# Pooled attention and a channel mix on one core: another way to take the row maximum from head 14 on, and six pieces of work on other engines

## The chip, the cores and the metric

The kernel runs on one core of a Trainium2 chip. The metric is the device time of one execution in microseconds; for the kernel before there are three runs. The profile is of one more execution, taken by the hardware profiler. TensorE does the matrix products (PE, and PEld for its weight loads), VectorE is DVE, ScalarE is ACT, GpSimd is POOL, and SyncE (SP) issues all transfers.

## The reference

Inputs: q, k, v of 8 batches x 8 heads x 1152 rows x 64, and the weights of a channel mix (512 x 1024, 1024 x 512, 512 x 512).

```
q_pool = q.reshape(B, H, S // 2, 2, D).mean(axis=3)          # 576 rows
scores = scale * q_pool @ k.T                                # 576 x 1152
attn = exp(scores - max(scores)); attn /= sum(attn) + 1e-9
x = (attn @ v), heads side by side                           # 8 x 576 x 512
xk = mu_k * x + (1 - mu_k) * x_prev ; xr likewise with mu_r
out = sigmoid(xr @ w_r) * ((relu(xk @ w_k) ** 2) @ w_v)
```

The result is wanted at float32 accuracy, so most operands are kept as two 16-bit parts, a high and a low one.

## The kernel before, in words

64 heads are taken one after the other; each is cut into 6 blocks of 96 pooled queries, 384 blocks in all. `prep` loads k and v of a head, splits k into a high and a low part (`kn`, L521 and L524), turns them by a DMA transpose into `ks1`, and copies the high part into the lower half of `ks2`. It also makes the parts of v (`vt`) and a scaled copy (`vb`, L552 on ScalarE for the first 8 heads, L555 on GpSimd after that).

A block (`block`, L562) has one of three PSUM buffers `s` of 1024 columns: 128 scratch columns and 9 x 96 scores, keys on the partitions, queries on the columns. Its steps:

1. 9 products with `ks1` (L583).
2. VectorE takes the maximum over the 9 key chunks, per partition and query (L590), to `mx`.
3. TensorE transposes `mx` by a product of 128 columns into the scratch (L593); VectorE takes the maximum over 128 keys (L595), to `mb`.
4. TensorE brings the 96 maxima back onto one row by a product with a diagonal (L602, 96 columns); ScalarE writes that row, pushed a little so that it bounds from above, into row 0 of the low part of q (L605).
5. 9 products with `ks2`, whose row 0 holds a constant and so subtracts the maximum (L599).
6. ScalarE's exponential, to `pf` (L611); GpSimd makes the low plane `pl` (L619).

`window` and `halves` multiply the planes with v (L640, L669, L671, L676) and divide by the row sums to `xb`. Two heads together are turned so that features lie on the partitions: for pairs 4 to 30 (`crossed`) GpSimd splits `xb` into 16-bit planes `xp` (L719), a DMA transposes them to `xd`, and ScalarE (first 64 tokens) and GpSimd (the rest) join them to `xt` (L730).

When a batch of 8 heads is done its channel mix follows (`ff`), in 18 tiles of 256 tokens over the whole run: `mix` makes the mixed tokens `xm` (L884), a high part on ScalarE (L889) and a low part on VectorE (L892), then come the products (L913; 256 columns against w_k, 512 against w_r and w_v), three for each pair of operands. The weights are decoded into two parts in the first 8 heads or so (`weights`, L772 to L802).

No loop sets the order of work. Every operation is entered into a list with an engine, a duration, what it reads and writes, and a key (`Issue.add`); a planner plays the list with these durations, sorts by the resulting start times, shifts some priorities at random by the seeds in `MOVES`, and issues every engine's work in that fixed order. So each engine runs its own queue in order, and the second half's products fill TensorE's time between blocks.

Of the kernel before, what the change touches and what calls it, by code (L numbers as in the profile page):

```python
# [11 lines left out]
F32 = mybir.dt.float32  # L12
# [25 lines left out]
EPS = 2.0 ** -10  # L38
ROW = "Prelu"
CROSS = range(4, 31)  # L40
SPLIT_ENG = "POOL"
JOIN_ENG = "POOL"
HALF_ENG = 'ACT'
CROSS_LOAD, CROSS_MORE = 2.1, 0.5


# [9 lines left out]

LATE, SLACK = 0.04, 0.05
KN_POOL = 0
XL_POOL = 0
DEC_K, DEC_RV = "V", "V"  # L60
ALT = 0
PL_ENG, PL_N = (), 0
VB_ACT = 8
HALF = 1.02
PE_T = 2
N_KN = 3
WR_AT = 5
WV_AT = 6
DEC_V = "Y"
# [14 lines left out]
WDEP = [("ks1", 1), ("ks2", 0), ("vr", 1)]  # L84
AHEAD2 = 0
MOVES, BASE, REACH = (
    19, 49, 186, 236, 290, 409, 442, 580, 720, 1033, 1106, 1276, 1618, 2283, 5078, 5201, 6339, 9039, 9106,
    9116, 10203, 12147, 12598, 14335, 15483, 18964, 19207, 19294, 19356, 20563, 27506, 27677, 27810,
), 2000000, 1150.0
SEED, SPREAD = 37, 1.0  # L90


class Issue:
# [1 line left out]
    LAT = {("PE", "DMA"): 0.2, ("PE", "PE"): 0.0,  # L95
           ("PE", "ACT"): 0.26, ("PE", "DVE"): 0.23, ("DVE", "PE"): 0.17, ("ACT", "PE"): 0.17,
           ("ACT", "POOL"): 0.18, ("DVE", "POOL"): 0.155, ("POOL", "PE"): 0.11, ("ACT", "DVE"): 0.142,
           ("DVE", "ACT"): 0.128, ("DVE", "DVE"): 0.12, ("ACT", "ACT"): 0.13, ("POOL", "POOL"): 0.13}
    ISSUED, LANDED, AHEAD = 1.2, 0.45, 8.0

    def __init__(self):
# [216 lines left out]
def kernel(  # L318
# [78 lines left out]
    xm = bufs("xm", 3, [P, T], F32)  # L397
# [32 lines left out]
    def later():  # L430
        for x, t_ in enumerate(ks2):
# [127 lines left out]

    BK = [(0, 4), (4, NC)]  # L560

    def block(n, j, i, t):  # L562
# [10 lines left out]
        mxz, mbz, y = mx[i % 2], mb[z], i % 2  # L573
# [12 lines left out]
        for c0, c1 in BK:  # L586
            op("PE", (c1 - c0) * 0.0430, lambda c0=c0, c1=c1: scores(c0, c1),
               r=[("ks1", hp), ("ks1", hp, 5)] + kh, w=[("s", z)], key=t)

        op("DVE", 0.975, lambda: nc.vector.tensor_reduce(mxz[:, P - QN:P], grid(0, NC).rearrange("p c q -> p q c"),  # L590
                                                         axis=AX.X, op=ALU.max),
           r=[("s", z)], w=[("mx", y)], key=t)
        op("PE", 0.059, lambda: nc.tensor.matmul(s[:, 0:P], mxz, identb, start=False, stop=False, skip_group_check=True),  # L593
           r=[("mx", y)], w=[("s", z)], key=t + O_MAX)
        op("DVE", 0.199, lambda: nc.vector.tensor_reduce(mbz, s[:, 0:P], axis=AX.X, op=ALU.max),  # L595
           r=[("s", z)], w=[("mb", z)], key=t + O_MAX)
# [5 lines left out]
        op("PE", 0.047, lambda: nc.tensor.matmul(s[:, 0:QN], mbz.broadcast_to([P, P]), negi[:, P - QN:P],  # L602
                                                 start=False, stop=False, skip_group_check=True),
           r=[("mb", z)], w=[("s", z)], key=t + O_MAX)
        op("ACT", 0.153, lambda: nc.scalar.activation(qlo[0:1], s[0:1, 0:QN], getattr(AF, ROW),  # L605
                                                      scale=1.0 - EPS, alpha=(1.0 + EPS) / (1.0 - EPS)),
           r=[("s", z)] + kl, w=qm, key=t + O_MAX)
        for c0, c1 in BK:
            op("PE", (c1 - c0) * 0.0430, lambda c0=c0, c1=c1: scores2(c0, c1),
               r=[("ks2", hp)] + kl + qm, w=[("s", z)], key=t + O_EXP)  # L610
        op("ACT", NC * QN / 1200 + 0.06, lambda: nc.scalar.activation(  # L611
            pf[:, :, rows], grid(0, NC), AF.Exp, bias=SHIFT, scale=0.125 / (2.0 * SQ)), r=[("s", z)], w=[("pf", x) for x in us] + [("gate", i)], key=t + O_EXP)
        pe = PL_ENG[i % len(PL_ENG)] if i < PL_N else "POOL"
        if pe == "ACT":
            op(pe, NC * QN / 1200 + 0.09, lambda: nc.scalar.activation(
                pl[:, :, rows], half(pf, U16, 0)[:, :, rows], AF.Copy, scale=LO), r=[("pf", x) for x in us], w=[("pl", x) for x in us], key=t + O_REST)
        else:
            en, d = (nc.gpsimd, NC * QN / 1000 + 0.12) if pe == "POOL" else (nc.vector, NC * QN / 1920 + 0.07)
            op(pe, d, lambda: en.tensor_scalar(  # L619
                pl[:, :, rows], half(pf, U16, 0)[:, :, rows], LO, 1.0, op0=ALU.mult, op1=ALU.mult),  # L620
               r=[("pf", x) for x in us], w=[("pl", x) for x in us], key=t + O_REST, port=True)
# [246 lines left out]
    def mix(w, t0, t1, key, dk, y):  # L868

        m, o = mu[w]  # L870
        n = t1 - t0
        for c in range(NG):
            t, zx = t0, turn("xm", 3)
            x_m, kx = xm[zx], [("xm", zx, False), ("xm", zx, True)]
            while t < t1:
                b = t // TQ
                e = min(t1, (b + 1) * TQ)
                x, s0, ln, o0 = xt[b % 3], t - b * TQ, e - t, t - t0
                z = turn("tmp")
# [113 lines left out]
    for n in range(B * H):  # L993
# [70 lines left out]
```

## Time and profile before

| | us |
|---|---|
| median of 3 runs | 1112.23 |
| lowest, highest | 1108.02, 1112.65 |
| profiled execution, its own time | 1112.57 |
| profiled execution, span from first to last instruction | 1110.4 |

The span is what the views of the profile divide; the 2.2 us beside it lie before the first and after the last instruction. An instruction's duration in a view is its own, from start to end. Neighbours on one engine can overlap, matmuls above all, whose ends are modelled, so a sum of durations can exceed an engine's busy time.

### The profile page before, as it was taken

To read this page: it belongs to the slowest core of one execution; us is meant where nothing else is said; L and a number is where in the kernel's file an instruction comes from. 1 tells how busy PE (TensorE), PEld (TensorE's weight loads), DVE (VectorE), ACT (ScalarE), POOL (GpSimd) and SP (SyncE) were. 2 spreads that over 40 slices of the span, in tenths; PEclk is the share of its full clock that TensorE was granted. 3 is DMA by queue.
4 is the path that set the end of the run, shared out by engine and by line. 5 is a ranking of instruction groups with operands and counts; after the bars stand their busy time and mean duration, and the time that the engine had idled before them with its cause. 6 is when DMAs were issued, how large, how long until landed. Compare 5 with 4: busy or idle time off the path is not lost.

```text
span 1110.4 us, 44176 instructions
## 1 busy us (share of the span) xinstructions
PE 1070.5 (96%) x18821; PEld 877.6 (79%) x18821; DVE 905.3 (82%) x1632; ACT 836.8 (75%) x1767; POOL 615.9 (55%) x632
## 2 busy tenths in 40 slices
PE   6778899999999999999999999999999999999998
PEld 5777788978798787988797978888797978787565
DVE  7998879988888988899988889897878888874530
ACT  7999987877877777777777777777777777766643
POOL 4656775764566563655565555655565656653111
PEclk9999999999999999999999999999999999999999
DMA  9997837464766655566576566756465554410000
GB/s 228 244 222 191 203 89 144 94 130 98 176 131 127 141 116 137 110 141 125 131 140 139 107 126 116 131 119 134 112 125 102 133 101 78 88 40 11 20 24 25
DMA packets 254165, 134.52 MB, mean 121 GB/s; under 512 B 189456, under 2 KB 226320, under 8 KB 253968
## 3 DMA queue, kind: packets, MB, share of 16 engines
q1 hardware_dynamic: 253968, 131.71, 55.6%
q8 instruction: 147, 2.41, 0.9%
q14 instruction: 50, 0.41, 0.1%
HBM read 67.11 MB, written 9.44 MB: 69 GB/s over the span
## 4 chain that ended last, share of the span: by engine, by line
PE 62%; DMA 2%; DVE 1%; ACT 1%; issue 1%; POOL 0%; SPq 0%; ACTq 0%; DVEq 0%
PE f L913 25%; PE s L583 8%; PE s L599 8%; PE s L913 4%; PE a L676 4%; PE a L671 4%; PE a L669 4%; PE a L913 2%; PE a L640 2%; PE s L593 1%; DMA ks<-kn 1%; DMA qT<-qn 1%; PE s L602 1%; ACT pf L611 1%; DVE mx L590 0%
## 5 line engine op out<-in xcount | busy, mean ns | idle before, releaser
L619 POOL TENSOR_SCALAR pl<-pf 128x864 f16<-128x864 uint16 x384 | 383.3, 998 | 320.8 <-ACT pf L611 264.6
L590 DVE TENSOR_REDUCE mx<-s 128x96 f16<-128x864 f32 x384 | 400.2, 1052 | 79.8 <-PE s L583 36.5
L611 ACT ACTIVATE pf<-s 128x864 int32<-128x864 f32 x384 | 335.4, 882 | 84.3 <-PE s L599 62.5
L583 PE MATMUL s<-qT,ks 128*128 128x96 f16 x3456 | 217.4, 207 | 15.1 <-ACT pf L611 14.0
L599 PE MATMUL s<-qT,ks 128*128 128x96 f16 x3456 | 212.5, 206 | 3.8 <-ACT qT L605 3.0
L583 PEld LDWEIGHTS <-ks 128*128 128x128 f16 x3456 | 182.2, 98 | 41.6 <-issue 19.2
L599 PEld LDWEIGHTS <-ks 128*128 128x128 f16 x3456 | 177.0, 98 | 23.7 <-issue 5.8
L671 PE MATMUL a<-vt,pf 128*128 128x64 f16 x2304 | 192.5, 194 | 0.0
L669 PE MATMUL a<-vt,pf 128*128 128x65 f16 x2304 | 192.0, 193 | 0.0
L669 PEld LDWEIGHTS <-pf 128*128 128x128 f16 x2304 | 161.9, 99 | 4.5
L671 PEld LDWEIGHTS <-pf 128*128 128x128 f16 x2304 | 155.1, 97 | 6.5
L605 ACT ACTIVATE qT<-s 1x96 f16<-1x96 f32 x384 | 88.1, 232 | 89.9 <-PE s L602 82.8
L913 PE MATMUL f<-xhk,wk_hi 128*128 128x256 f16 x496 | 135.2, 273 | 1.0 <-ACT r L940 0.5
L913 PE MATMUL f<-xhk,wk_lo 128*128 128x256 f16 x496 | 135.2, 273 | 0.0
L913 PE MATMUL f<-xlk,wk_hi 128*128 128x256 f16 x496 | 135.2, 273 | 0.0
L595 DVE TENSOR_REDUCE mb<-s 128x1 f16<-128x128 f32 x384 | 108.4, 285 | 31.0 <-PE s L593 27.2
L944 POOL TENSOR_TENSOR gl<-g 128x512 f16<-128x512 f32 x72 | 77.9, 1082 | 84.6 <-ACT g L942 70.1
L676 PE MATMUL a<-vb,pl 128*128 128x65 f16 x2304 | 124.3, 193 | 0.0
L913 PEld LDWEIGHTS <-wk_hi 128*128 128x128 f16 x1152 | 105.5, 98 | 11.4 <-issue 1.2
L676 PEld LDWEIGHTS <-pl 128*128 128x128 f16 x2304 | 98.7, 98 | 5.4
L913 PE MATMUL f<-wv_hi,g 128*128 128x512 f16 x240 | 91.0, 379 | 0.0
L913 PE MATMUL f<-wv_hi,gl 128*128 128x512 f16 x240 | 90.9, 379 | 0.0
(119 smaller groups left out, 2028.8 us busy)
## 6 DMA issues: line engine op xcount, KB each, us to landing
kr<-in_k_dram SPq DMA_DIRECT2D x64, 288.0 KB
vr<-in_v_dram SPq DMA_DIRECT2D x64, 288.0 KB
qr<-in_q_dram SPq DMA_DIRECT2D x63, 256.0 KB
ks<-ks SPq DMA_DIRECT2D x64, 144.0 KB
out_dram<-em SPq DMA_DIRECT2D x36, 256.0 KB
xt<-in_moe_w_k_dram SPq DMA_DIRECT2D x8, 512.0 KB
xt<-in_moe_w_v_dram SPq DMA_DIRECT2D x8, 512.0 KB
qr<-in_q_dram SPq DMA_DIRECT2D x32, 64.0 KB
```

What stands on the lines that cost most here:

```text
L583: nc.tensor.matmul(cols(c, c + 1), ks1[hp][:, c, :], qhi, start=(c == c0), stop=False, skip_group_check=True)
L590: op("DVE", 0.975, lambda: nc.vector.tensor_reduce(mxz[:, P - QN:P], grid(0, NC).rearrange("p c q -> p q c"), axis=AX.X, op=ALU.max), r=[( ...
L595: op("DVE", 0.199, lambda: nc.vector.tensor_reduce(mbz, s[:, 0:P], axis=AX.X, op=ALU.max), r=[("s", z)], w=[("mb", z)], key=t + O_MAX)
L599: nc.tensor.matmul(cols(c, c + 1), ks2[hp][:, c, :], qlo, start=False, stop=True, skip_group_check=True)
L605: op("ACT", 0.153, lambda: nc.scalar.activation(qlo[0:1], s[0:1, 0:QN], getattr(AF, ROW), scale=1.0 - EPS, alpha=(1.0 + EPS) / (1.0 - EPS) ...
L611: op("ACT", NC * QN / 1200 + 0.06, lambda: nc.scalar.activation(pf[:, :, rows], grid(0, NC), AF.Exp, bias=SHIFT, scale=0.125 / (2.0 * SQ)) ...
L619: op(pe, d, lambda: en.tensor_scalar(pl[:, :, rows], half(pf, U16, 0)[:, :, rows], LO, 1.0, op0=ALU.mult, op1=ALU.mult), r=[("pf", x) for ...
L669: nc.tensor.matmul(bank[:, a0:a0 + VN], half(pf, F16, 1)[:, c, rows], vt[jv][:, c, D:D + VN], start=(w == 1 and c == 0 and hh == 0), stop= ...
L671: nc.tensor.matmul(bank[:, a0:a0 + D], half(pf, F16, 1)[:, c, rows], vt[jv][:, c, 0:D], start=False, stop=False, skip_group_check=True)
L676: nc.tensor.matmul(bank[:, a0:a0 + VN], pl[:, c, rows], vb[jv][:, c, 0:VN], start=False, stop=(c == NC - 1), skip_group_check=True)
L913: nc.tensor.matmul(ps, terms[i][0], terms[i][1], start=(first and i == 0), stop=(i == last), skip_group_check=True)
L944: op("POOL", 2 * n * 0.00203 + 0.08, lambda f2=f2: nc.gpsimd.tensor_tensor(gl[:, f2, 0:n], g32[:, f2, 0:n], gh[:, f2, 0:n], op=ALU.subtrac ...
```

## The change

From head 14 on (`N_ROW = 14`) steps 2 to 4 of a block are replaced. VectorE takes the maximum with 32 x 32 transposition over each group of 32 queries in one instruction (`top`), which leaves for each group of 32 partitions the maximum over its 32 keys. `join` then does the rest: a maximum over the key chunks (9 numbers to 3), a product with a mask that spreads the four partition groups over 6 columns, one TensorE product of 18 columns with the constant `gather`, which brings the four groups onto 32 partitions, a maximum over two windows of 5 columns (the maximum and its positive part), and VectorE's 32 x 32 transposition straight into rows 0 to 31 of the low part of q. `ks2` now has a constant in rows 0 and 1; ScalarE's step is gone in these blocks. Heads 0 to 13 keep the old steps with the new constants.

Besides: the split and the joins of `crossed` are on ScalarE (`SPLIT_ENG`, `JOIN_ENG`); the scaled v of all heads is on ScalarE (`VB_ACT`); the low parts of the mixed tokens are on GpSimd (`XL_POOL`); `kn` has two buffers (`N_KN`); the fills of `ks2` are done by VectorE at the start and no longer by GpSimd under a key; the planner gets a few other durations, another seed and other moves. `PAIR = 99` means that the joining of two blocks at once is not used.

```diff
-SPLIT_ENG = "POOL"
-JOIN_ENG = "POOL"
+N_ROW = 14
+PAIR = 99
+SPLIT_ENG = 'ACT'
+JOIN_ENG = 'ACT'
...
-XL_POOL = 0
+XL_POOL = 9999
-VB_ACT = 8
-HALF = 1.02
+VB_ACT = 99
+HALF = 0.92
+XM_D = 0.126
-N_KN = 3
+N_KN = 2
...
-SEED, SPREAD = 37, 1.0
+SEED, SPREAD = 7, 1.0
...
+    mask = const.tile([P, 6], F32, name="mask")
+    gather = const.tile([P, P // U, U], F16, name="gather")
+    nc.vector.memset(mask, 0.0)
+    for a in range(P // U):
+        part = slice(a * U, (a + 1) * U)
+        nc.vector.memset(mask[part, a + 1:a + 2], 1.0 / SM)
+        nc.gpsimd.tensor_copy(gather[part], ident[part, part].unsqueeze(1).broadcast_to([U, P // U, U]))
+    nc.vector.memset(mask[0:U, 0:1], 1.0 / SM)
...
-            op("POOL", 0.6, lambda t_=t_: nc.gpsimd.memset(t_[0:D], 0.0), w=[("ks2z", x)], key=60.0)
-            op("POOL", 0.9, lambda t_=t_: nc.gpsimd.memset(t_[0:1], SM), w=[("ks2z", x), ("ks2", x)], key=60.0)
+    for t_ in md:
+        nc.gpsimd.memset(t_, 0.0)
+    for t_ in ks2:
+        nc.vector.memset(t_[0:D], 0.0)
+        nc.vector.memset(t_[0:2], -SM * 2.0 * EPS)
+        nc.vector.memset(t_[0:1], -SM * (1.0 - EPS))
...
+        def top(y, a):
+            op("DVE", 0.972, lambda: nc.vector.tensor_reduce(
+                my[y][:, a], cols(0, NC).rearrange("p (x q) -> p x q", q=U), axis=AX.X, op=ALU.max, apply_transpose=True),
+               r=[("s", z)], w=[("my", y)], key=t)
+
+        def join(y, m):
...
+            op("DVE", 0.062 + 0.028 * m, lambda: nc.vector.tensor_reduce(
+                mr.rearrange("p (a j) -> p a j", j=3), my[y][:, 0:m].rearrange("p a (c j) -> p a j c", j=3), axis=AX.X, op=ALU.max),
+               r=[("my", y)], w=[("s", z)], key=t + O_MAX)
+            op("DVE", 0.061 + 0.019 * m, lambda: nc.vector.tensor_tensor(
+                mqz, mr.unsqueeze(2).broadcast_to([P, 3 * m, 6]), mask.unsqueeze(1).broadcast_to([P, 3 * m, 6]), op=ALU.mult),
+               r=[("s", z)], w=[("mq", y)], key=t + O_MAX)
+            op("PE", GA, lambda: nc.tensor.matmul(s[:, U:U + 18 * m], gather.rearrange("p a x -> p (a x)"),
+                                                  mqz.rearrange("p j k -> p (j k)"), start=False, stop=False, skip_group_check=True),
+               r=[("mq", y)], w=[("s", z)], key=t + O_MAX)
+            op("DVE", 0.055 + 0.031 * m, lambda: nc.vector.tensor_reduce(
+                md[y][:, 0:3 * m, 0:2], windows(got, 5), axis=AX.X, op=ALU.max), r=[("s", z)], w=[("md", y)], key=t + O_MAX)
+            op("DVE", 0.072 + 0.1 * m, lambda: nc.vector.transpose(ql, md[y][:, 0:3 * m].rearrange("p j x -> p (j x)")),
+               r=[("md", y)] + kls, w=qms, key=t + O_MAX)
...
+    def blocks(n, j):
+        i = n * NB + j
+        if n < N_ROW:
+            first, row, _, _, second = block(n, j, i, i * PER)
+            first()
+            row()
+            second()
+        elif n < PAIR:
+            first, _, top, join, second = block(n, j, i, i * PER)
+            first()
+            top(i % 2, 0)
+            join(i % 2, 1)
+            second()
```

## Rows read from the trace of the kernel before

**Rows 1.** The page: busy us (share of the span) and instructions of each engine.

```profile
PE 1070.5 (96%) x18821; PEld 877.6 (79%) x18821; DVE 905.3 (82%) x1632; ACT 836.8 (75%) x1767; POOL 615.9 (55%) x632
```

**Rows 2.** Windows: length, busy PE, PEld, DVE, ACT, POOL; clock, DMA share, GB/s.

```profile
0.00:100.00 100.00, 74.67 (x1594) 65.96 (x1595) 87.69 (x163) 88.42 (x191) 56.83 (x65) 1.00 1.02 226
100.00:150.00 50.00, 45.09 (x943) 40.46 (x943) 43.88 (x80) 49.23 (x112) 37.08 (x37) 1.00 0.71 182
150.00:1000.00 850.00, 844.20 (x15419) 702.56 (x15417) 733.58 (x1311) 641.83 (x1344) 501.64 (x512) 1.00 0.57 118
1000.00:1110.40 110.40, 106.56 (x874) 68.58 (x870) 40.19 (x80) 57.29 (x122) 20.30 (x21) 1.00 0.05 20
```

**Rows 3.** Chain of work that ended last, 385 to 408 us: start, us, what.

```profile
384.96 0.06 PE s L593
...
385.23 0.04 PE s L602
385.28 0.65 PE f L913 x3
...
390.96 6.23 DMA ks<-kn
...
400.12 0.03 PE a L671
...
400.91 0.22 PE f L913 x2
```

**Rows 4.** Line L611, the exponentials: durations min/median/max ns, first and last start.

```profile
L611 ACT ACTIVATE pf<-s x384: 862/891/910, 14.0 to 1012.4; 128x864 int32<-128x864 f32 x192
```

**Rows 5.** Groups by line and shape: busy us, mean ns | idle before, releasers.

```profile
L590 DVE TENSOR_REDUCE mx<-s 128x96 f16<-128x864 f32 x384 | 400.2, 1052 | 79.8 <-PE s L583 36.5 <-ACT pf L611 9.9 <-ACT qT L605 7.1
...
L595 DVE TENSOR_REDUCE mb<-s 128x1 f16<-128x128 f32 x384 | 108.4, 285 | 31.0 <-PE s L593 27.2 <-PE s L602 1.2
...
L605 ACT ACTIVATE qT<-s 1x96 f16<-1x96 f32 x384 | 88.1, 232 | 89.9 <-PE s L602 82.8 <-DVE vt L544 1.6 <-DVE mb L595 1.4
L593 PE MATMUL s<-identb,mx 128*128 128x128 f16 x384 | 83.6, 220 | 4.5 <-DVE mx L590 4.2
L602 PE MATMUL s<-negi,mb 128*128 128x96 f16 x384 | 78.7, 207 | 5.0 <-DVE mb L595 4.5
```

**Rows 6.** Timeline of VectorE, 380 to 388 us: start, us, engine, line.

```profile
384.27 0.28 DVE L595 TENSOR_REDUCE mb<-s 128x1 f16<-128x128 f32 x1
384.47 0.15 DVE L692 TENSOR_SCALAR den<-a 128x4 f32<-128x4 f32 x1
384.54 0.34 DVE L884 SCALAR_TENSOR_TENSOR xm<-xt,mu_r,tmp 128x128 f32<-128x128 f32 x1
```

**Rows 7.** Groups by line and shape: work that is moved, and its nearest neighbours.

```profile
L892 DVE TENSOR_TENSOR xlr<-xm,xhr 128x256 f16<-128x256 f32 x72 | 41.3, 586 | 2.0 <-ACT xhr L889 1.9
...
L555 POOL TENSOR_SCALAR vb<-vr 128x576 f16<-128x576 f32 x56 | 40.5, 723 | 41.8 <-PE a L676 20.0 <-PE a L640 14.2 <-PE s L593 4.2
...
L730 POOL COPY xt<-xd 128x1024 uint16<-128x1024 uint16 x27 | 37.1, 1376 | 7.1 <-DMA xd<-xp 6.0
...
L892 DVE TENSOR_TENSOR xlk<-xm,xhk 128x256 f16<-128x256 f32 x72 | 36.1, 510 | 17.3 <-ACT xhk L889 17.3
L473 ACT ACTIVATE qn<-qs 128x1152 f16<-128x1152 f32 x31 | 35.8, 1154 | 1.1 <-DMA qT<-qn 1.1
L719 POOL COPY xp<-xb 128x1152 uint16<-128x1152 uint16 x27 | 34.3, 1271 | 10.2 <-DVE xb L701 9.3
...
L802 POOL TENSOR_TENSOR wv_lo<-ex,wv_hi 128x512 f16<-128x512 f32 x8 | 10.3, 1282 | 1.2 <-ACT wv_hi L801 0.9
...
L552 ACT ACTIVATE vb<-vr 128x576 f16<-128x576 f32 x8 | 5.4, 673 | 0.0
```

**Rows 8.** Timeline of the first microseconds: a fill, and VectorE's first split of k.

```profile
4.22 1.05 POOL L433 MEMSET ks<- 1x1152 f16 x1
...
5.06 0.85 DVE L524 TENSOR_TENSOR kn<-kr,kn 128x256 f16<-128x256 f32 x2 [3.94 <-ACT kn L521]
```

More of the change, by code (lines that the diff above doesn't have):

```diff
@@ L40 @@
 CROSS = range(4, 31)
-SPLIT_ENG = "POOL"
-JOIN_ENG = "POOL"
-HALF_ENG = 'ACT'
+N_ROW = 14
+PAIR = 99
+GA = 0.045
+XM = 3
+SPLIT_ENG = 'ACT'
+JOIN_ENG = 'ACT'
+HALF_ENG = "ACT"
 CROSS_LOAD, CROSS_MORE = 2.1, 0.5
@@ L97 @@
            ("ACT", "POOL"): 0.18, ("DVE", "POOL"): 0.155, ("POOL", "PE"): 0.11, ("ACT", "DVE"): 0.142,
-           ("DVE", "ACT"): 0.128, ("DVE", "DVE"): 0.12, ("ACT", "ACT"): 0.13, ("POOL", "POOL"): 0.13}
+           ("DVE", "ACT"): 0.128, ("DVE", "DVE"): 0.14, ("ACT", "ACT"): 0.13, ("POOL", "POOL"): 0.13}
     ISSUED, LANDED, AHEAD = 1.2, 0.45, 8.0
@@ L392 @@
     mx, mb = bufs("mx", 2, [P, P], F16), bufs("mb", 3, [P, 1], F16)
+    my, mq = bufs("my", 2, [P, 2, 3 * NC], F32), bufs("mq", 2, [P, 6, 6], F16)
+    md = bufs("md", 2, [U, 6, U], F16)
     den, xb = bufs("den", 2, [P, NW], F32), bufs("xb", 1, [P, 2 * NW, D], F32)
@@ L560, with windows @@
     BK = [(0, 4), (4, NC)]
+    def windows(x, n):
+        return bass.AP(tensor=x.tensor, offset=x.offset, ap=[*x.ap[0:2], [1, 2], [1, n]])
     def block(n, j, i, t):
@@ L584, in scores @@
                                  start=(c == c0), stop=False, skip_group_check=True)
[L586 to L596, printed above, removed]
+        def first():
+            for c0, c1 in BK:
+                op("PE", (c1 - c0) * 0.0430, lambda c0=c0, c1=c1: scores(c0, c1),
+                   r=[("ks1", hp), ("ks1", hp, 5)] + kh, w=[("s", z)], key=t)
@@ new lines, in row @@
+        def row():
+            mxz, mbz, y = mx[i % 2], mb[z], i % 2
+            op("DVE", 0.975, lambda: nc.vector.tensor_reduce(mxz[:, P - QN:P], grid(0, NC).rearrange("p c q -> p q c"),
+                                                             axis=AX.X, op=ALU.max),
+               r=[("s", z)], w=[("mx", y)], key=t)
+            op("PE", 0.059, lambda: nc.tensor.matmul(s[:, 0:P], mxz, identb, start=False, stop=False, skip_group_check=True),
+               r=[("mx", y)], w=[("s", z)], key=t + O_MAX)
+            op("DVE", 0.199, lambda: nc.vector.tensor_reduce(mbz, s[:, 0:P], axis=AX.X, op=ALU.max),
+               r=[("s", z)], w=[("mb", z)], key=t + O_MAX)
+            op("PE", 0.047, lambda: nc.tensor.matmul(s[:, 0:QN], mbz.broadcast_to([P, P]), negi[:, P - QN:P],
+                                                     start=False, stop=False, skip_group_check=True),
+               r=[("mb", z)], w=[("s", z)], key=t + O_MAX)
+            op("ACT", 0.153, lambda: nc.scalar.activation(qlo[0:1], s[0:1, 0:QN], getattr(AF, ROW),
+                                                          scale=(1.0 + EPS) / (1.0 - EPS), alpha=(1.0 - EPS) / (1.0 + EPS)),
+               r=[("s", z)] + kl, w=qm, key=t + O_MAX)
@@ new lines, in top @@
+        def top(y, a):
[3 more added lines that the diff above has]
+        def join(y, m):
+            ql = qT[qi][0:U, 1].rearrange("p j x -> p (j x)")[:, q0 + QN - m * QN:q0 + QN]
+            kls = kl if m == 1 else [("qTl", qi, c) for c in range((q0 - QN) // P, (q0 + QN - 1) // P + 1)]
+            qms = [("qm", qi, q0 - x * QN) for x in range(m)]
+            mr, got = s[:, 0:3 * m], s[0:U, U:U + 18 * m].rearrange("p (j k) -> p j k", k=6)
+            mqz = mq[y][:, 0:3 * m]
+            op("DVE", 0.062 + 0.028 * m, lambda: nc.vector.tensor_reduce(
[11 more added lines that the diff above has]
+               r=[("md", y)] + kls, w=qms, key=t + O_MAX)
@@ L600, in scores2 @@
                                  start=False, stop=True, skip_group_check=True)
[L602 to L619, printed above, removed]
+        def second():
+            for c0, c1 in BK:
+                op("PE", (c1 - c0) * 0.0430, lambda c0=c0, c1=c1: scores2(c0, c1),
+                   r=[("ks2", hp)] + kl + qm, w=[("s", z)], key=t + O_EXP)
+            op("ACT", NC * QN / 1200 + 0.06, lambda: nc.scalar.activation(
+                pf[:, :, rows], grid(0, NC), AF.Exp, bias=SHIFT, scale=0.125 / (2.0 * SQ)),
+               r=[("s", z)], w=[("pf", x) for x in us] + [("gate", i)], key=t + O_EXP)
+            op("POOL", NC * QN / 1000 + 0.12, lambda: nc.gpsimd.tensor_scalar(
@@ L620, in block @@
                 pl[:, :, rows], half(pf, U16, 0)[:, :, rows], LO, 1.0, op0=ALU.mult, op1=ALU.mult),
                r=[("pf", x) for x in us], w=[("pl", x) for x in us], key=t + O_REST, port=True)
+        return first, row, top, join, second
+    def blocks(n, j):
[11 more added lines that the diff above has]
+            second()
+        elif j % 2 == 0:
+            y = i // 2 % 2
+            one, two = (block(n, j + x, i + x, (i + x) * PER) for x in range(2))
+            for x, (first, _, top, _, _) in enumerate((one, two)):
+                first()
+                top(y, x)
+            two[3](y, 2)
+            one[4]()
+            waiting.append(two[4])
+        else:
+            waiting.pop()()
@@ L623 @@
+    waiting = []
     VN = D + 1
@@ L872, in mix @@
         for c in range(NG):
-            t, zx = t0, turn("xm", 3)
+            t, zx = t0, turn("xm", XM)
             x_m, kx = xm[zx], [("xm", zx, False), ("xm", zx, True)]
@@ L883, in mix @@
    r=xk + [("omu", w)], w=[("tmp", z)], key=key + c * dk)
-                op("DVE", ln / 960 + 0.069, lambda x=x, s0=s0, ln=ln, o0=o0, z=z, c=c, x_m=x_m: nc.vector.scalar_tensor_tensor(
+                op("DVE", ln / 960 + XM_D, lambda x=x, s0=s0, ln=ln, o0=o0, z=z, c=c, x_m=x_m: nc.vector.scalar_tensor_tensor(
                     x_m[:, o0:o0 + ln], x[:, c, s0 + 1:s0 + 1 + ln], m[:, c:c + 1], tmp[z][:, 0:ln],
@@ L981, in ff @@
         return key
-    later()
     queries(0, -20.0)
@@ L1001 @@
             i = n * NB + j
-            block(n, j, i, i * PER)
+            blocks(n, j)
             if i == WR_AT * NB:
```

13 lines of the change are left out of this document (5 added, 8 removed).

## The prediction

> **What bounds the kernel now.** I read the page first, then busy time by stretch. The page gives TensorE 96% of the span and the other three 55 to 82% [rows 1]; but its matmul ends are modelled, so that alone proves nothing. The stretches do more [rows 2]: from 150 us to 1000 us TensorE is idle for 5.8 of 850 us and in the last 110 us for 3.8, while in the first 150 us it is idle for 30.2. The granted clock is 1.00 in each, which is the 2.4 GHz level. VectorE is busy 86% of the long stretch, ScalarE 76%, GpSimd 59%.
>
> The chain of waits shows whether the busy TensorE is really at work [rows 3]. There its pieces follow one another at what their columns take: three 512-column products in 0.65 us, two 256-column ones in 0.22 us, which is 0.43 ns a column; a 64-column one in 0.03 us. So after 150 us the kernel is bound by TensorE's columns, not by a latency: a column removed there is time removed. The attention half supplies scores and windows, the second half (L913) fills what is left; the last exponential starts at 1012.4 us [rows 4] and 97 us of TensorE work stand behind it.
>
> Before 150 us it is otherwise: ScalarE is busy 49.2 of 50 us between 100 and 150 [rows 2], and the DMA share is about 1 up to 100. There nothing that TensorE is spared comes back.
>
> **TensorE's part.** Blocks of heads 14 to 63, 50 x 6 = 300 of 384, lose the 128-column transposing product (L593) and the 96-column broadcast (L602) and get one gather of 18 columns. By columns the two take 128 x 0.43 = 55 ns and 96 x 0.43 = 41 ns; the chain shows 0.06 and 0.04 [rows 3]. The rows' own means, 220 and 207 ns [rows 5], are latencies that overlap and are not the price. The gather has no row. Below, 18 columns at 0.43 ns are 8 ns; above, it costs as much as the product it resembles, 60 ns. The nearest row is a 64-column product with its own weight load, 30 ns, and I take that, since the 128-wide weight load stays. Saved: 55 + 41 - 30 = 66 ns a block, 19.8 us in all; with the bounds 26.4 and 10.8 us.
>
> One rule speaks to that unknown. The Trainium skill, "TensorE: Matmul & The Clock Gate", section "Wait — 56ns, not 53.3ns?", says that successive matmuls never start closer than about 25 ns, however few the columns. No row of this case has so few columns; by that figure the gather costs 25 ns and the sum would be 21.3 us saved, an estimate.
>
> Head 14 begins at block 84; with 384 blocks in the 998 us from 14.0 to 1012.4 [rows 4], 2.6 us each, that is about 230 us, so all 300 lie where TensorE is the bound.
>
> **VectorE's part.** The maximum reads the same 864 PSUM columns as L590, 1052 ns [rows 5]. It now transposes in passing, and no row shows such an instruction: below, the same 1052; above, half the rate, 1052 + 900. I take 1052. The second maximum (285 ns on 128 columns) gives way to four small instructions: maximum over 9 columns, product of 18, maximum over 30, transposition of 96. From L692, 150 ns on 4 columns, and L595, 285 on 128 [rows 5, 6], one column is worth 1.05 ns and these show about 155, 165, 180 and 250, together 750. But on this engine the next instruction starts early: L692 0.20 us after L595's start, L884 0.07 us after L692's [rows 6], some 80 ns inside the shown time. As slots the four take 430 ns against 205: +225 ns a block, 68 us. If each has to wait out the one in front, 750 - 205 = +545 ns, 164 us. Off go 144 subtractions for the low parts, 72 each for the two mixes, 586 and 510 ns [rows 7], as slots 468: -67 us. Net between +1 and +97 us on VectorE.
>
> What hides this is the order of the two halves. The second half is 1728 products of 256 columns and 1296 of 512 (18 tiles; 96, and 72 of the wider), 0.11 and 0.217 us each [rows 3]: 471 us, 59 us for a batch. Behind the last exponential TensorE has 97 us, 38 more than the last batch itself needs. So the attention can end 38 us later against TensorE's end before TensorE starves; TensorE's end comes 20 us earlier, which leaves 18 us over 300 blocks, 2.66 us each. VectorE's work per block in the long stretch is 733.6 us over its 850/2.6 = 327 blocks, 2.24 us; the subtractions were 67 us over some 350 blocks, 0.19 each; the new one is 2.24 + 0.225 - 0.19 = 2.28 at best and 2.60 at worst. It holds, with little room at the upper end.
>
> **ScalarE's and GpSimd's parts.** ScalarE loses 300 biases of 232 ns [rows 5], 70 us. It gets 27 splits, of 1152 and 128 elements, and 27 joins of 1024. Its 1152-element copy takes 1154 ns and its 576-element one 673 [rows 7], so the three are about 1150, 300 and 1050: 67.5 us; and 56 scaled v at 673 ns, 37.7 us. Net +35 us, from 75% to 80% of the span. GpSimd loses the same copies (27 of 1271 and of 1376 ns, 71.5 us, the small ones not counted) and v (723 ns, 40.5 us) and gets 144 subtractions at half of L802's 1282 ns on 512 columns [rows 7]: +92, net -20 us. What each is now queued behind: a low part behind a plane of about 1 us on GpSimd, then the product that reads it; an exponential behind a split of 1.15 us on ScalarE, then the plane, the windows and the third score buffer. Both engines have idle time where these lie, and TensorE has other products meanwhile; without that cover each split or join would cost TensorE about 1 us, 50 us in all. I cost it at nothing, except once: three or so pairs of heads lie before head 14, without the saved biases. Where ScalarE is full, between 100 and 150 us, they add three v and at most one split and join, 2 to 4.5 us; a share reaches TensorE: +1.5 us, between 0 and 4.
>
> **Start.** The fills of ks2 move from GpSimd to the front of VectorE, now six instead of four, and the mask's small ones. On GpSimd one of 1152 columns took 1.05 us [rows 8]. Six at that price are 6.3 us from about 1.1 us on, where VectorE's first split of k starts at 5.06 us [rows 8]: 2.4 us late at most, and TensorE, DMA and ScalarE wait behind it; zero at least, if fills are quicker there. I take +1.5 us. The gather's constants go to GpSimd, which loses 4 us of fills in the same place.
>
> **Edits at nothing.** Two kn buffers for three: the transposing load took 6.2 us [rows 3] and a head lasts 6 x 2.6 = 15.6 us, so the buffer is free again in time; if not, its copy slips by part of 6 us, once a head, behind filler products. The planner's own durations, seed and moves change the order alone. A static order with four in-engine dependences more will leave some stalls beyond the 5.8 us of the long stretch: +1 us.
>
> **Sum.** The profiled execution took 1112.6 us, 2.2 outside its span; the median of the runs, 1112.2, lies 0.3 below. 1112.6 - 19.8 + 1.5 + 1.5 + 1 = 1096.8; against the median 1096.5 us.
>
> **Rivals.**
> - *VectorE's chain takes back half* (1103 to 1113 us). The four links stand in one queue behind 0.9 us splits and maxima, and with all waits VectorE needs 2.60 us of the 2.66 that there are. For it: 86% busy already [rows 2]. Against it: two of the present links, TensorE and ScalarE, fall out, and subtractions leave. Half of the 19.8 us back gives 1106 or so.
> - *More than the sum* (1083 to 1090). The gather costs 8 ns (-6.6 us) and the new order finds some of the 30 us idle before 150 us. Against it: ScalarE and DMA are full there.
> - *The change doesn't do what it says* (1107 to 1117): the spared columns turn into idle time because something behind TensorE, such as ScalarE's exponentials, sets the pace. Against it: back-to-back pieces in the chain.
> - *Slower: the transposing maximum reads at less than the plain one's rate.* It decides from where VectorE's block exceeds 2.66 us, so from 2.66 - 2.28 = 0.38 us more than L590, 1.43 us shown. At half rate it is +0.90, 3.18 us a block: 300 x 3.18 from 230 us on is 1184, and 59 for the last batch: about 1245 us. No row excludes it. The Trainium skill, "Vector Engine (DVE) Microarchitecture Reference", section "3.8 The reshape front-end and per-opcode configuration", speaks against this rival: the 32x32 transposing front end is pipelined to one element per cycle and lane. No run yet shows it.
>
> **Chances.** My sum within its bounds (1090 to 1103): 0.60. VectorE takes back: 0.15. More: 0.11. No effect: 0.07. Slower: 0.07. The range 1085 to 1113 leaves out the slow case, a part of the third and an end of the first: some 0.16. What this kernel's measurement tells from no change is about 0.5%, 5.6 us. Faster by more, under 1106.7: 0.60 + 0.11 + half of the second = 0.78; within: the other half and most of no effect, 0.14; slower: 0.08.
>
> **What would show it.** Right: granted clock 1.00, TensorE still idle for under 15 us after 150 us, matmul count lower by 300, the gather's pieces 0.03 us in the chain, the new maximum near 1.05 us, its four links under 0.25 us each, exponentials ending near 1000 to 1015 us and less than 97 us behind them. Wrong: a maximum above 1.4 us; TensorE waiting on VectorE by tens of us; first score product later than 8.3 us by more than 2.5; idle time before 150 us well above 30.

## The result, and the profile after

| | before | changed |
|---|---|---|
| median, us | 1112.44 (4 runs, 1108.02 to 1113.82) | 1096.07 (4 runs, 1093.44 to 1099.84) |
| ratio, 95% interval | | 0.9868, 0.9836 to 0.9900 |
| profiled execution: span, us | 1110.4 | 1094.8 |
| mean granted clock of its TensorE | 1.000 | 0.995 |

Forecast were 1096.5 us and a range of 1085 to 1113; the change is faster by 16.4 us. Below, "the changed kernel" is the one with the change and "the kernel before" the one without. First the busy times of the changed kernel, from its page, beside [rows 1]:

```profile
PE 1052.2 (96%) x18521; PEld 858.5 (78%) x18521; DVE 920.7 (84%) x2400; ACT 878.2 (80%) x1604; POOL 593.6 (54%) x641
```

300 matmuls fewer, as it should be (two go, one comes), VectorE 15 us busier, ScalarE 41 us, GpSimd 22 us less. The windows, with the columns of [rows 2]:

```profile
0.00:100.00 100.00, 75.65 (x1575) 66.24 (x1575) 87.49 (x171) 85.68 (x185) 52.72 (x67) 0.97 0.97 216
100.00:150.00 50.00, 44.95 (x888) 40.95 (x889) 43.61 (x75) 49.57 (x116) 35.66 (x37) 0.97 0.80 185
150.00:1000.00 850.00, 840.65 (x15477) 696.00 (x15475) 763.68 (x2113) 696.55 (x1208) 477.00 (x504) 1.00 0.59 119
1000.00:1094.80 94.80, 90.94 (x586) 55.34 (x584) 25.90 (x43) 46.46 (x100) 28.19 (x35) 1.00 0.06 23
```

TensorE's shown idle time is nearly as before: 29.4 us up to 150 us (30.2 before), 9.4 up to 1000 (5.8), 3.9 behind (3.8). New is the granted clock, 0.97 in the first two rows where the kernel before showed 1.00. What took the place of [rows 5], groups by line and shape:

```profile
L627 DVE TRANSPOSE_TENSOR_REDUCE my<-s 128x27 f32<-128x864 f32 x300 | 319.9, 1072 | 48.7 <-PE s L602 35.9 <-ACT pf L660 2.9 <-PE s L643 2.7
...
L648 DVE STREAM_TRANSPOSE qT<-md 32x96 f16<-32x96 f16 x300 | 75.1, 255 | 2.1
...
L637 DVE TENSOR_REDUCE s<-my 128x3 f32<-128x27 f32 x300 | 53.7, 184 | 1.6
...
L643 PE MATMUL s<-mq,gather 128*128 128x18 f16 x300 | 49.9, 173 | 1.7 <-DVE mq L640 1.7
...
L646 DVE TENSOR_REDUCE md<-s 32x6 f16<-32x30 f32 x300 | 47.0, 160 | 15.1 <-PE s L643 13.3
L640 DVE TENSOR_TENSOR mq<-s,mask 128x18 f16<-128x18 f32 x300 | 45.6, 156 | 1.9
```

The transposing maximum takes 1072 ns where the plain one took 1052. The four links show 184, 156, 160 and 255 ns, 755 together, 750 forecast; the wait for the gather, ahead of L646, is 13 us over all 300 blocks. In VectorE's timeline of this kernel (start, us), beside [rows 6], they follow one another far closer than they are long:

```profile
605.50 0.17 DVE L637 TENSOR_REDUCE s<-my 128x3 f32<-128x27 f32 x1
605.57 0.25 DVE L648 STREAM_TRANSPOSE qT<-md 32x96 f16<-32x96 f16 x1
605.76 0.12 DVE L640 TENSOR_TENSOR mq<-s,mask 128x18 f16<-128x18 f32 x1
605.82 0.17 DVE L637 TENSOR_REDUCE s<-my 128x3 f32<-128x27 f32 x1
605.91 0.73 DVE L540 TENSOR_TENSOR kn<-kr,kn 128x576 f16<-128x576 f32 x1
```

The links of two blocks are interleaved, and the slots (from one start to the next) are 0.07, 0.19, 0.06 and 0.09 us. The moved work, beside [rows 7]:

```profile
L568 ACT ACTIVATE vb<-vr 128x576 f16<-128x576 f32 x64 | 43.7, 682 | 0.0
...
L964 POOL TENSOR_TENSOR xlr<-xm,xhr 128x256 f16<-128x256 f32 x72 | 51.1, 714 | 33.5 <-ACT xhr L961 19.0 <-DVE em L1049 4.2 <-DVE xm L956 4.0
L964 POOL TENSOR_TENSOR xlk<-xm,xhk 128x256 f16<-128x256 f32 x72 | 50.7, 712 | 23.1 <-ACT xhk L961 16.2 <-DVE xm L956 4.5
...
L802 ACT COPY xt<-xd 128x1024 uint16<-128x1024 uint16 x27 | 36.7, 1359 | 1.3 <-DMA xd<-xp 1.2
...
L791 ACT COPY xp<-xb 128x1152 uint16<-128x1152 uint16 x27 | 31.2, 1155 | 2.7 <-DVE xb L773 2.6
```

The split is at its forecast 1150 ns, the join at 1359 and not 1050, a low part at 713 and not 641. TensorE's waits show none of that. The largest one for ScalarE, for a score buffer that an exponential holds, was longer before the change (total us, times, longest us; before, then changed):

```profile
PE s L583 <- ACT pf L611: 14.0, 23, 1.6
```

```profile
PE s L602 <- ACT pf L660: 10.6, 25, 1.1
```

**The clock.** The windows around three places in the first 150 us show what the kernel before did not have in its profiled execution (columns as above):

```profile
43.00:49.00 6.00, 3.63 (x52) 2.70 (x49) 4.72 (x9) 6.00 (x13) 2.73 (x3) 1.00 1.16 204
49.00:53.00 4.00, 3.35 (x48) 3.26 (x48) 3.38 (x5) 3.45 (x8) 1.38 (x2) 0.57 1.37 192
53.00:57.00 4.00, 4.00 (x123) 4.00 (x121) 2.92 (x5) 1.60 (x5) 2.52 (x3) 1.00 0.99 318
71.00:77.00 6.00, 3.74 (x57) 2.86 (x57) 5.03 (x8) 6.00 (x16) 3.13 (x4) 0.99 0.74 224
77.00:81.00 4.00, 3.79 (x55) 3.41 (x53) 3.07 (x7) 3.73 (x9) 2.38 (x2) 0.59 1.26 174
...
125.00:128.00 3.00, 1.64 (x26) 1.40 (x27) 2.41 (x4) 3.00 (x12) 1.49 (x3) 1.00 0.75 84
128.00:132.00 4.00, 3.78 (x55) 3.44 (x52) 3.27 (x6) 3.84 (x9) 1.82 (x2) 0.57 0.57 176
```

Ahead of each fall ScalarE is busy all the time and TensorE for 3.63 of 6, 3.74 of 6 and 1.64 of 3 us; then the clock stands at the 1.2 GHz level for most of 4 us, in which TensorE is busy for 3.35 to 3.79 and does less than half as much (48 matmuls, and 123 in the 4 us behind the first). The three cost 4 x (0.43 + 0.41 + 0.43) = 5.1 us of full-clock time.

What brings the clock down is not shown. The profiled execution of the kernel before has a stretch as thin, with ScalarE as full, and kept the full clock (first row); and the same kernel without its shifts (run 6 below) falls too (second row):

```profile
69.00:75.00 6.00, 3.39 (x54) 2.62 (x54) 5.55 (x11) 6.00 (x17) 2.98 (x4) 1.00 0.72 193
```

```profile
76.00:80.00 4.00, 4.00 (x65) 3.83 (x65) 2.37 (x5) 3.52 (x7) 2.20 (x3) 0.58 0.94 180
```

### The profile page after: what moved, and what is told of

Its sections match the earlier page's. It is cut to its first block, busy times and chain, and to the rows that moved or that the text cites. A ratio compares the mean times of both kernels' runs of the same rounds, so it can differ in the third digit from the quotient of the medians.

```text
span 1094.8 us, 43933 instructions
## 1 busy us (share of the span) xinstructions
PE 1052.2 (96%) x18521; PEld 858.5 (78%) x18521; DVE 920.7 (84%) x2400; ACT 878.2 (80%) x1604; POOL 593.6 (54%) x641
## 4 chain that ended last, share of the span: by engine, by line
PE 82%; ACT 5%; DVE 5%; DMA 2%; issue 2%; POOL 0%; ACTq 0%; DVEq 0%
PE f L985 34%; PE s L602 11%; PE s L653 11%; PE a L748 5%; PE a L743 5%; PE a L741 5%; PE s L985 5%; ACT pf L660 2%; PE a L712 2%; PE a L985 2%; DMA ks<-kn 2%; DVE my L627 1%; ACT xt L802 1%; DVE mx L612 1%; DVE xm L956 1%
## 5 line engine op out<-in xcount | busy, mean ns | idle before, releaser
L627 DVE TRANSPOSE_TENSOR_REDUCE my<-s 128x27 f32<-128x864 f32 x300 | 319.9, 1072 | 48.7 <-PE s L602 35.9
L612 DVE TENSOR_REDUCE mx<-s 128x96 f16<-128x864 f32 x84 | 87.3, 1052 | 16.3 <-PE s L602 5.6
L985 PE MATMUL f<-wv_lo,g 128*128 128x512 f16 x240 | 90.9, 379 | 0.0
```

The costliest lines, as they stand in the source:

```text
L627: op("DVE", 0.972, lambda: nc.vector.tensor_reduce(my[y][:, a], cols(0, NC).rearrange("p (x q) -> p x q", q=U), axis=AX.X, op=ALU.max, app ...
L985: nc.tensor.matmul(ps, terms[i][0], terms[i][1], start=(first and i == 0), stop=(i == last), skip_group_check=True)
```

## The experiments

All beside runs of the kernel before on the same chip, whose medians were 1112.75 (runs 1 to 4), 1111.44 (5 to 8) and 1111.87 us (9 to 12); each ratio is to these.

**1. Fills on GpSimd.**

```diff
-        nc.vector.memset(t_[0:D], 0.0)
-        nc.vector.memset(t_[0:2], -SM * 2.0 * EPS)
-        nc.vector.memset(t_[0:1], -SM * (1.0 - EPS))
+        nc.gpsimd.memset(t_[0:D], 0.0)
+        nc.gpsimd.memset(t_[0:2], -SM * 2.0 * EPS)
+        nc.gpsimd.memset(t_[0:1], -SM * (1.0 - EPS))
```

> The changed kernel with the six fills of ks2 at the start on GpSimd instead of VectorE; every engine's order is otherwise that of the changed kernel. There VectorE's first split of k begins at 7.98 us where it began at 5.06 before the change, and TensorE's first score product at 10.63 us instead of 8.34. Theory A (the late start is a cost that stays): first split near 5 us again, first scores near 8.3, total 1.5 to 3 us below the changed kernel's 1096, so 1093 to 1094.5. Theory B (the first 150 us are set by DMA and ScalarE and absorb it): first split near 5 us, total within 1 us of 1096. Either way the granted clock is the second thing to look at: A and B say nothing of it, and if it comes out at 1.00 the time should be lower by a further 5 us.

Measured: 1096.36 us (4 runs), ratio 0.9845, 0.9819 to 0.9870; clock 0.993 to 0.996. VectorE's first split of k and the first score products, in the timelines of the changed kernel and of this one:

```profile
7.98 0.47 DVE L540 TENSOR_TENSOR kn<-kr,kn 128x320 f16<-128x320 f32 x1
...
10.63 0.64 PE L602 MATMUL s<-qT,ks 128*128 128x96 f16 x6 [0.55 <-ACT qT L520]
```

```profile
4.24 0.49 DVE L540 TENSOR_TENSOR kn<-kr,kn 128x320 f16<-128x320 f32 x1 [2.64 <-ACT kn L537]
...
8.12 1.60 PE L602 MATMUL s<-qT,ks 128*128 128x96 f16 x18 [1.76 <-ACT qT L520]
```

The late start is real and goes away, 2.5 us at the first product, but the median does not follow: theory B in its number. The intervals of the two ratios overlap, so a cost of 0 to some 3 us is left open.

**2. The gather three times.**

```diff
-            op("PE", GA, lambda: nc.tensor.matmul(s[:, U:U + 18 * m], gather.rearrange("p a x -> p (a x)"),
-                                                  mqz.rearrange("p j k -> p (j k)"), start=False, stop=False, skip_group_check=True),
+            def gathers():
+                for x0 in (U, 2 * U, 3 * U):
+                    nc.tensor.matmul(s[:, x0:x0 + 18 * m], gather.rearrange("p a x -> p (a x)"),
+                                     mqz.rearrange("p j k -> p (j k)"), start=False, stop=False, skip_group_check=True)
+            op("PE", GA, gathers,
```

> The changed kernel with the 18-column gather issued three times in each of the 300 blocks, the two additional ones into unused scratch columns; order and planner's durations unchanged. Theory A (TensorE's columns are the bound after 150 us, and a gather costs the 0.027 us that is its mean start-to-start distance in the trace): 600 x 0.027 = 16 us more than the changed kernel, 1112. Theory B (small products hide in gaps of TensorE, and the gain came from something other than its columns): less than 4 us more, 1096 to 1100. If the gather cost as much as the 128-column product, 0.055 each, it would be 33 us more, 1129.

Measured: 1106.89 us (5 runs), ratio 0.9952, 0.9930 to 0.9974; 10.8 us over the changed kernel. TensorE's timeline of this run, at two blocks:

```profile
600.26 0.22 PE L645 MATMUL s<-mq,gather 128*128 128x18 f16 x3
600.34 0.19 PE L745 MATMUL a<-vt,pf 128*128 128x65 f16 x1
...
601.46 0.22 PE L645 MATMUL s<-mq,gather 128*128 128x18 f16 x3
601.53 0.38 PE L989 MATMUL f<-wr_lo,xhr 128*128 128x512 f16 x1
```

From the start of three to the next start it is 0.08 and 0.07 us. Over the long stretch 0.08 is the usual value, 27 ns for one, so 600 take 16 us; 10.8 came through, 18 ns each. A product of TensorE costs time even if it is that small: theory A, at two thirds of its number.

**3. Filler products in the first heads.**

```diff
+            if c1 == NC and n < 10:
+                for _ in range(6):
+                    nc.tensor.matmul(s[:, 0:P], zeros, identb, start=False, stop=False, skip_group_check=True)
```

> The changed kernel with six additional products of 128 zero columns in each block of heads 0 to 9, right behind the first score products (60 blocks x 6 x 0.055 = 20 us of TensorE work in a stretch where TensorE is idle for about 30 us). The profile of the changed kernel shows the granted clock at 0.5 in three places between 49 and 131 us, which the kernel before does not have; mean 0.995, and its four runs go from 0.997 at 1093.4 us to 0.992 at 1099.8. Theory A (the low clock costs TensorE about 5 us): clock back to 0.998 or more and 1090 to 1094 us, as long as the products land in idle time. Theory B (the low clock falls in a stretch that TensorE does not bound, so it costs nothing): clock back, time unchanged or up to 5 us longer, 1096 to 1101. If the clock stays at 0.995 nothing follows but the price of the products.

Measured: 1105.25 us (4 runs), ratio 0.9925, 0.9908 to 0.9941; clock 0.998 to 1.000. Its windows:

```profile
0.00:150.00 150.00, 125.19 (x2684) 114.60 (x2685) 125.73 (x234) 130.05 (x282) 83.49 (x99) 1.00 0.87 201
150.00:1000.00 850.00, 841.19 (x15448) 697.28 (x15446) 761.16 (x2111) 697.98 (x1212) 479.48 (x505) 1.00 0.59 120
```

The clock is back, and the kernel is 9.2 us slower: outside both expectations. The products did not land in idle time. Of their 20 us the idle time took up 5 (TensorE's total is now 1066.3 of 1104.1 us, 37.8 idle against 42.6); 15 would have been added, the span grew by 9.3, and the 5.7 between them is about what the full clock gave back. That last step is a sum and not a measurement: it rests on 0.055 us for each product and on busy times whose ends are modelled.

**4. More work on VectorE.**

```diff
+                nc.vector.tensor_reduce(dump[y], cols(0, 2), axis=AX.X, op=ALU.max)
```

> The changed kernel with one more VectorE instruction in each of the 300 blocks, a plain maximum over 192 PSUM columns right behind the transposing one, its result unused: 0.20 us of slot each, 60 us in all; order unchanged. VectorE is busy 764 of the 850 us between 150 and 1000. Theory A (my prediction's count: VectorE's block grows from 2.33 to 2.53 us, under the 2.66 from which it would decide): within 6 us of the changed kernel, below 1102. Theory B (the order is fixed, so what VectorE loses TensorE waits for): 20 to 60 us more, 1116 to 1156.

Measured: 1130.90 us (4 runs), ratio 1.0162, 1.0137 to 1.0186; 34.8 us over the changed kernel. The page, and the added instruction as a group:

```profile
PE 1071.9 (95%) x18521; PEld 863.1 (77%) x18521; DVE 995.4 (88%) x2700; ACT 882.9 (78%) x1604; POOL 597.9 (53%) x641
...
L631 DVE TENSOR_REDUCE dump<-s 128x1 f32<-128x192 f32 x300 | 94.3, 314 | 0.0
```

VectorE's busy time is up by 75 us (995.4 less 920.7), 0.25 us a block and not the 0.20 expected. Line of the exponentials, in the changed kernel, in this one and in run 9 (count, durations, first and last start):

```profile
L660 ACT ACTIVATE pf<-s x384: 863/891/932, 16.0 to 999.2; 128x864 int32<-128x864 f32 x192
```

```profile
L665 ACT ACTIVATE pf<-s x384: 862/891/924, 16.4 to 1032.2; 128x864 int32<-128x864 f32 x192
```

```profile
L660 ACT ACTIVATE pf<-s x384: 860/891/931, 16.1 to 994.3; 128x864 int32<-128x864 f32 x192
```

Spans are 1094.8, 1127.9 and 1090.0: from the last exponential's start to the end it is 95.6, 95.7 and 95.7 us. The attention ended 33 us later and nothing of the second half had been drawn into the gaps meanwhile. Theory B. The added instruction stands in front of the links, so it lengthens each block's chain as well as VectorE's load; which of the two TensorE waited for was not separated, here or in run 9.

**5 and 6. Both kernels without the shifts.**

```diff
-MOVES, BASE, REACH = (
...
-), 2000000, 1150.0
+MOVES, BASE, REACH = (), 2000000, 1150.0
```

> The changed kernel with the planner's list of random shifts left empty, so its order is the planner's own. Beside it runs the kernel before, treated alike. Theory A (the gain is TensorE's spared columns): both get slower by what the shifts were worth, and the difference between the two stays 12 to 24 us. Theory B (the gain is the new order): the difference goes to under 5 us.

> The kernel before with the planner's list of random shifts left empty. Theory A (the gain is TensorE's spared columns): 12 to 24 us above the changed kernel treated alike. Theory B (the gain is the new order): within 5 us of it.

Measured: changed 1095.73 us (4 runs), ratio 0.9854, 0.9837 to 0.9872; before 1112.91 (10 runs), ratio 1.0015, 0.9997 to 1.0033. Neither list of shifts is worth anything that can be measured on its own kernel, and the difference stays 17.2 us: theory A.

**7. The new maximum alone.**

```diff
-SPLIT_ENG = 'ACT'
-JOIN_ENG = 'ACT'
+SPLIT_ENG = 'POOL'
+JOIN_ENG = 'POOL'
...
-XL_POOL = 9999
+XL_POOL = 0
...
-VB_ACT = 99
+VB_ACT = 8
```

> The changed kernel with all four pieces of moved work back where they were: splits and the second join on GpSimd, scaled v from head 8 on GpSimd, low parts of the tokens on VectorE. The new maximum stays; the planner orders anew with the changed kernel's shifts. VectorE then has 2.33 + 0.19 = 2.52 us of work a block against the 2.66 from which it would decide. Theory A (the spared columns are the whole gain, the moved work only gives room): 1094 to 1104 us. Theory B (without the subtractions gone VectorE sets the pace): above 1110.

Measured: 1134.36 us (4 runs), ratio 1.0203, 1.0186 to 1.0219; clock 0.992 to 0.995. Slower than before by 23 us: theory B in its number. But part of the loss lies where the new maximum is not yet in use, ahead of head 14 (about 230 us):

```profile
0.00:150.00 150.00, 114.57 (x2352) 102.36 (x2353) 131.01 (x240) 129.48 (x281) 81.40 (x96) 0.94 0.88 205
```

Up to 150 us it is some 110 matmuls behind the changed kernel, whose two windows hold 2463.

**8. The moved work alone.**

```diff
-N_ROW = 14
+N_ROW = 64
```

> The changed kernel with the old maximum in all 64 heads: only the moved work, the fills, the two kn buffers and the planner's settings are new. Theory A (the spared columns are the gain): no faster than the kernel before, 1110 to 1120 us, with ScalarE at 85% of the span since it keeps its 300 biases. Theory B (the moved work or the settings bring the gain): below 1104.

Measured: 1125.17 us (4 runs, 1121.15 to 1129.90), ratio 1.0133, 1.0097 to 1.0170. That excludes theory B and is 5 us above theory A's range. Neither part on its own gains, with the caution on orders below.

**9. Less work on VectorE.**

```diff
-                my[y][:, a], cols(0, NC).rearrange("p (x q) -> p x q", q=U), axis=AX.X, op=ALU.max, apply_transpose=True),
+                my[y][:, a, 0:18], cols(0, 6).rearrange("p (x q) -> p x q", q=U), axis=AX.X, op=ALU.max, apply_transpose=True),
...
-                mr.rearrange("p (a j) -> p a j", j=3), my[y][:, 0:m].rearrange("p a (c j) -> p a j c", j=3), axis=AX.X, op=ALU.max),
+                mr.rearrange("p (a j) -> p a j", j=3), my[y][:, 0:m, 0:18].rearrange("p a (c j) -> p a j c", j=3), axis=AX.X, op=ALU.max),
```

> The changed kernel with the transposing maximum reading 6 of the 9 key chunks (576 of 864 columns) in the 300 blocks, so the maximum is left out over a third of the keys; order unchanged. It takes some 0.30 us off VectorE in each block, 90 us in all, and shortens each block's chain by as much. The run with 60 us more on VectorE was 35 us slower, 0.58 us for each us. Theory A (the changed kernel stands at TensorE's columns, VectorE has just enough room): at most 6 us below 1096, since TensorE's shown idle time after 150 us is 9 us before 1000 and 4 behind. Theory B (VectorE sets part of the pace at all loads, at 0.58): 15 us or more below, 1081 or less.

Measured: 1089.84 us (4 runs), ratio 0.9804, 0.9782 to 0.9826; 6.2 us under the changed kernel. Its page, and its maximum as a group:

```profile
PE 1052.1 (97%) x18521; PEld 860.2 (79%) x18521; DVE 838.6 (77%) x2400; ACT 877.6 (81%) x1604; POOL 588.0 (54%) x641
...
L627 DVE TRANSPOSE_TENSOR_REDUCE my<-s 128x18 f32<-128x576 f32 x300 | 232.2, 776 | 82.6 <-PE s L602 62.8 <-PE s L643 5.2 <-ACT pf L660 3.9
```

VectorE is busy for 82 us less (838.6 against 920.7), of which 6 come through, where 75 us more had cost 35: theory A, at the end of its range.

**10 to 12. One part at a time, or one more.** Run 10 has the `XL_POOL` line of run 7's diff alone, run 11 the other three lines, and run 12:

```diff
-QS_POOL = 0
+QS_POOL = 64
```

> The changed kernel with only the tokens' low parts back on VectorE (144 subtractions, 67 us of slot); splits, joins and scaled v stay on ScalarE. With all four pieces back the kernel took 1134. Theory A (the subtractions on VectorE are what cost there): 67 x 0.58 = 39 us more than the changed kernel, 1125 to 1140. Theory B (GpSimd's load with splits, joins and v was the cost): within 8 us of 1096.

> The changed kernel with splits, second join and scaled v (from head 8) back on GpSimd and the low parts on GpSimd too: GpSimd rises from 54% to about 65% of the span, ScalarE falls from 80% to about 73%. Theory A (VectorE's subtractions were the cost with all four pieces back): within 8 us of 1096. Theory B (GpSimd's queue was): above 1115.

> The changed kernel with the sums of query pairs (31 x 838 ns) also on GpSimd: VectorE loses 26 us, GpSimd gets about 40. The planner orders anew. Theory A (TensorE's columns are the bound, VectorE has just enough room): within 5 us of 1096, on either side. Theory B (VectorE paces at 0.58 us for each us): 15 us below, 1081.

| | median, us | ratio, 95% interval |
|---|---|---|
| 10: low parts on VectorE | 1132.68 | 1.0186, 1.0165 to 1.0207 |
| 11: planes and v on GpSimd | 1120.86 | 1.0084, 1.0063 to 1.0105 |
| 12: query sums on GpSimd too | 1120.55 | 1.0082, 1.0055 to 1.0109 |

Run 10 agrees with A in its number, run 11 with B, and run 12 with neither: it takes 26 us of sums off VectorE and is 24 us slower. The windows of run 12, up to 150 us and to 1000 us:

```profile
0.00:150.00 150.00, 117.23 (x2436) 104.98 (x2437) 128.62 (x232) 132.54 (x292) 97.33 (x111) 0.95 0.90 207
150.00:1000.00 850.00, 828.34 (x15049) 680.85 (x15046) 737.17 (x2042) 684.24 (x1183) 491.69 (x515) 1.00 0.57 119
```

VectorE and ScalarE are less busy than in the changed kernel over the long stretch, GpSimd little more, and TensorE has done 428 matmuls fewer in it. No engine's load explains that. What runs 7, 8 and 10 to 12 have in common is that the planner ordered another list of operations with shifts drawn for the changed kernel's; runs 1 to 4 and 9 kept its order, 5 and 6 had no shifts. So part of each of these, some 24 us if they are all like run 12, may be the order and not the edit. That was not tried with an empty list and stays open. Between themselves low parts on VectorE cost 13.5 us beside planes on GpSimd (7 less 11) and 12.1 beside planes on ScalarE (10 less 12, which differ in the query sums as well); planes and v on GpSimd beside low parts on VectorE 1.7 us (7 less 10). Each of them was ordered anew, though, and these differences are smaller than run 12's 24 us, so they can be order as well.

Only run 9, which leaves a third of the maximum out, is clearly below the changed kernel; no run points to a version that would be.

## Why the prediction was right

**TensorE's columns: right.** The term was 66 ns a block, 19.8 us. The gather's price, taken at 30 ns between 8 and 60, is 27 ns by the distances of run 2, so 55 + 41 - 27 = 69 ns, 20.7 us. The 25 ns floor that the prediction cites from the Trainium skill, "TensorE: Matmul & The Clock Gate", section "Wait — 56ns, not 53.3ns?", is as near, and these distances agree with it. Runs 5 and 6 show that the gain does not hang on the shifts, run 2 that even the smallest product is paid for. No run puts the two old products back beside the new maximum, so their 55 and 41 ns are a sum that fits and not a measurement of their own.

**The three small losses: near in sum, wrong in kind, and in that lucky.** I added 1.5 us for the start, 1.5 for ScalarE between 100 and 150 us, 1 for stalls, 4.0 together. 20.7 less the 15.6 us between the two spans leaves 5.1 us lost. The three stretches at 1.2 GHz hold 5.1 us, and no step of the prediction had them: it looked at the clock of the kernel before, found 1.00, and carried that over. TensorE's idle time, where the three losses were to show, grew by 3.6 us in the long stretch, where 1 was forecast, and fell by 0.8 before it, where 3 were. The start is 2.3 us late at the first product, close to the 2.4 given as the most, and run 1 cannot tell whether it costs anything. That the numbers meet so well is more than two spans can bear: executions of the kernel before at one and the same clock, 0.998, took from 1107.4 to 1115.0 us beside runs 5 to 8.

How much of the low clock is paid in time is open too. In the changed kernel's four runs 0.997, 0.995, 0.995 and 0.992 go with 1093.4, 1095.5, 1096.6 and 1099.8 us; in run 8's, 0.997, 0.996, 0.993 and 0.989 with 1121.2, 1122.4, 1128.0 and 1129.9. That is 1.1 to 1.3 us for each 0.001, as much as if every lost column were paid (0.001 of the span is 1.1 us). But these are two of the closer cases. Within each of the twelve versions of the changed kernel it is 0.8 us on average, and in two of them nothing. The kernel before is not free of it either: 0.996 to 1.000 beside the runs and mostly 0.998, so that some 2 us of the 5.1 fall away in a comparison of medians. That the clock fell because ScalarE held TensorE back there was not tried, and the row of the kernel before at 69 us speaks against it as the whole reason.

**VectorE: the outcome right, its reason wrong.** The step "So the attention can end 38 us later against TensorE's end before TensorE starves" failed. Run 4 raised VectorE's block by 0.25 us, under the 0.38 from which by that step it would decide, and lost 35 us, because the 96 us behind the last exponential stayed as they were: the order is fixed when the kernel is built, and what stands behind the last block stays there. So VectorE's load could have been off by little only. The forecast held all the same since the links took 755 ns against 750, the transposing maximum 1072 against 1052, and the subtractions left: VectorE's busy time rose by 15 us, near the low end of the +1 to +97 forecast. Runs 4 and 9 put the changed kernel at the bend: 75 us more on VectorE cost 35, 82 less give 6. (One reading is slightly off: by L692 and L595, which the prediction names, a column is 1.09 ns and not 1.05; the links change by under 5 ns each.)

**The moved work.** I costed it at nothing but 1.5 us between 100 and 150 us. In the changed kernel nothing of it shows, and runs 7 and 8 show each half without the other slower than before; how much of that is their order is open. That the subtractions have to leave VectorE fits the 12 to 13.5 us between these runs and the 35 us of run 4, but their own price is not shown.

**The rivals.** "VectorE's chain takes back half" did not come, but run 4 shows how near it was. "More than the sum" did not come either: the gather was near its middle price and none of the idle time was won. "The change doesn't do what it says" is excluded by the time and by run 2. The slower one is excluded: the transposing maximum takes 1072 ns, the plain one 1052, and between 576 and 864 columns, 776 and 1072 ns, a column takes 1.03 ns. With that agrees the sentence that the prediction cites from the Trainium skill, "Vector Engine (DVE) Microarchitecture Reference", section "3.8 The reshape front-end and per-opcode configuration": one element per cycle and lane.

## What to carry to other kernels

Where the chain of waits shows one engine's pieces back to back, cost an edit by the distance between starts, not by durations shown: here two products of "220 and 207 ns" counted for 55 and 41. Where the order is fixed beforehand, work that stands behind the last stage is no reserve for an engine ahead of it; its slack is its own idle time in the stretch, and VectorE at 90% of the long stretch had next to none. And read the granted clock in several executions, not in one profile: 1.00 in the profile of the kernel before was 0.996 to 1.000 in its other runs and 0.992 to 0.997 in the changed kernel's.

## What the runs showed of the hardware that was not expected

- The granted clock fell to the 1.2 GHz level three times in 150 us, at 1.7 us of lost time each, after stretches in which TensorE was busy for 55 to 62% in pieces. A stretch of 57% in the kernel before (3.39 of 6 us) kept the full clock, so the share alone does not tell; with filler products in the same heads the clock was 0.998 to 1.000.
- The same fixed work gives different busy times: in run 4 TensorE shows 1071.9 us busy for the same 18521 matmuls that show 1052.2 in the changed kernel, at the same mean clock of 0.995. Single matmuls are as long in both (the score products 207 ns); they overlap less, so more of their latency counts as busy, and shown idle time understates waiting.
- VectorE's fills that overlap on one buffer left 0.29 us between them, so six fills of 0.54 to 1.02 us took 6.4 us; one of them:

```profile
2.31 1.02 DVE L449 MEMSET ks<- 2x1152 f16 x1 [0.29 <-DVE ks L448]
```

- Two 16-bit copies on ScalarE: the join of 1024 elements, which writes every second word, took 1359 ns, the split of 1152, which reads every second word, only 1155.
